# Windowed local attention in a fused attention, mixture-of-heads and MLP kernel: blocks of 64 (or 48) queries against sub-blocks of 32 queries by 64 keys in three of four batches

## Chip, cores and metric

One core of a Trainium2 chip runs the whole program. The metric is the device time of one execution in microseconds (us); the time of a kernel is the median of its runs.

## What is computed

The reference has three stages, all in float32. Only the first is touched here.

```python
def _attn_ref(q, k, v):                      # 4 batches, 8 heads, 576 positions, 64 channels
    scores = scale * np.matmul(q, k.transpose(0, 1, 3, 2))
    rel = pos[:, None] - pos[None, :]
    mask_plain = (rel >= 0) & (rel < 32)                      # heads 0 to 3
    mask_dil = (rel >= 0) & (rel < 128) & (rel % 4 == 0)      # heads 4 to 7
    scores = np.where(mask, scores, -1e9); attn = softmax(scores)
    return np.matmul(attn, v)
```

Its output, 4 x 576 x 512, goes through a layer of four causal heads, of which two per token are kept by a gate (`_moe_ref`), and then through a normalized MLP of width 2048 (`_moe2_ref`).

A plain head looks at the last 32 positions. A dilated head splits the 576 positions into 4 classes (position modulo 4) of 144, and within a class looks at the last 32 as well. So both kinds are a band 32 wide, and a block of n queries needs n + 32 keys.

## The kernel before

**Layout.** Heads are worked in pairs (`hp` 0 to 3; 0 and 1 plain, 2 and 3 dilated), one head on partitions 0 to 63 and the other on 64 to 127. For each batch and pair (16 in all), `load_qk` and `load_v` (L340, L364) issue DMAs from SP, `turned_qk` (L438) turns q and k by TensorE transposes into `qT` and `kT`, `scores` (L491) fills two PSUM banks, and two chains of `window` (L527), one per half `u` of the blocks, do the rest.

**Blocks.** Plain: 9 blocks of 64 queries by 96 keys, five in half 0 and four in half 1. Dilated: 12 blocks of 48 queries by 80 keys, six in each half. A block's scores lie on 64 partitions per head, so a half has 128 partitions by (blocks x keys) columns: 480, 384 or 480.

**Scores (L502 to L525).** First the mask is written into the bank by a bfloat16 product with the identity (L507, L512, L513), then q times k is added (L521). The stationary operand is 64 x 64 (or 64 x 48), and four tiles of the 128 x 128 array are used in turn: two row halves (the heads) by two column halves. Every float32 product appears as two records in the trace, so a plain pair has 36 records on L521 and a dilated one 48.

**Softmax and output (`window`).** For each half: a maximum (L542), exponentials in small ACT instructions, one per block (L551), or by a DVE addition and one large ACT instruction (L545, L548), a sum (L554), a reciprocal (L556), a product (L558, on DVE or POOL), one TensorE transpose per block (L570) in groups of up to four, each group into one bank and copied out by ACT or DVE to `pT` (L573), then the product with v (L587). There the stationary operand is v, 96 x 64 or 80 x 64, the moving one 64 or 48 columns, and the two heads use the two column halves of the array. Last, the result is split into a rounded part `xh` and a rest `xl` (L601, L603).

**Order.** All work is written as chains of Python generators; `run_chains` (L205) picks at each step the operation that could start first by its own table of costs and books it on an engine. So the order of instructions on every engine is fixed when the program is built, and a change of block sizes or of booked costs re-orders work of other stages too. An operation can be offered to two engines (`either`). On PE it books 128 ns more when the tile mode changes (L237). Buffers are places that are taken (`acq`) and given back (`give`): two of `sc` and one of `pT` per half, two of `vt`, eight banks.

**Stages.** Batch 0's local attention fills the first 40 us. From about 48 to 221 us the local attention of batches 1 to 3 is interleaved with the gated heads (`value_tile` L611, `project` L700, `attend` L774) and `out_proj` (L928) of the batch before. The MLP starts when the local attention of batch 3 is done (`open_mlp` L986): its weights are decoded from 221 us on, beside the last gated heads, and from about 320 us its products (L1181, L1203) fill PE.

Of the kernel before, what the change touches and what calls it, by code (L numbers as in the profile page):

```python
# [7 lines left out]
F32 = mybir.dt.float32  # L8
# [9 lines left out]
NEG = -1.0e30  # L18
# [5 lines left out]
def windowed_attention_moe_mlp(  # L24
# [38 lines left out]
    SCALE = 0.125  # L63
    DQ, DW = 48, 80
    LEAN = 0.0
    NBD = S // DQ

    def qrange(i):
# [76 lines left out]
    nc.vector.tensor_copy(mfirst, mgen)  # L145
    nc.vector.memset(mdil[:, 0, 0:W], NEG)
    nc.vector.memset(mfirst[:, 0:W], NEG)

    tri = const.tile([P, E, E], F32, name="tri")
    nc.gpsimd.memset(tri, 1.0)  # L150
# [21 lines left out]
    def acq(tag, n=1):  # L172
        return "acq", tag, n
# [138 lines left out]
    left = {}  # L312
    places.update(nat=[0.0] * 2, vt=[(0.0, LENT), (0.0, 0)], qT=[0.0] * 2, xh=[0.0] * XB)
    for u in range(NU):
        places["sc", u], places["pT", u] = [0.0] * 2, [0.0]
    land = [0.0]

    def last(k, n):
# [42 lines left out]
        LD[b, hp] = nats, times  # L361
        put("ld", b, hp, at=0.0)

    def load_v(b, hp, engines=("SP",)):  # L364
        h0 = 2 * hp
        dil = h0 >= H // 2
        if b == 0 and not dil:
            t, home = 0.0, None
            vt = late(f"vt{b}_{hp}", F32)
        else:  # L370
            t, home = (0.0, 8) if b == 0 and hp == NHP // 2 else (yield acq("vt"))
            if home:
                vt = x2a[:, home:home + 3].rearrange("p a n -> p (a n)")
            else:
                vt = win.tile([P, NBD * 2 * D], F32, tag="vt", name=f"vt{b}_{hp}")
        yield op("POOL", 250.0, [t])
        jobs = []
        if not dil:
            vt = vt[:96, :NBK * 2 * D].rearrange("p (t h d) -> p t h d", t=NBK, h=2)
            nc.gpsimd.memset(vt[0:W, 0], 0.0)  # L380
            jobs.append((32.0, vt[W:96, 0], v[b, h0:h0 + 2, 0:64].rearrange("h p d -> p h d")))
            for h in range(2):
                vs = v[b, h0 + h]
                jobs.append((192.0, vt[:, 1:, h], bass.AP(tensor=vs.tensor, offset=vs.offset + (64 - W) * D,
                                                          ap=[[D, 96], [64 * D, NBK - 1], [1, D]])))
        else:
            vt = vt[:DW, :NBD * 2 * D].rearrange("p (h c n) -> p h c n", h=2, c=3)
            nc.gpsimd.memset(vt[0:W, :, 0], 0.0)
            jobs.append((60.0, vt[W:DW, :, 0], v[b, h0:h0 + 2, 0:4 * DQ].rearrange("h (p r) d -> p h (r d)", r=4)))
            for h in range(2):  # L390
                vs = v[b, h0 + h]
                jobs.append((100.0, vt[:, h, 1:], bass.AP(tensor=vs.tensor, offset=vs.offset + 4 * (DQ - W) * D,
                                                         ap=[[4 * D, DW], [4 * DQ * D, 2], [1, 4 * D]])))
        tv = 0.0
        for x, (kb, dst, src) in enumerate(jobs):
            ns = 800.0 if x == 0 else 660.0
# [85 lines left out]
        put("qT", b, hp, at=max(ends))  # L482


    SC = {u: [win.tile([P, NBD // NU, 97], F32, name=f"sc{u}{x}") for x in range(2)] for u in range(NU)}
    for sx in SC[0] + SC[1]:
        nc.gpsimd.memset(sx[:, :, 96:], 1e-9)
    PSC = {}
    DBLK = (range(0, NBD // 2), range(NBD // 2, NBD))

    def scores(b, hp):  # L491
# [35 lines left out]
    def window(b, hp, u):  # L527

        t = yield key("s1", b, hp)
        tx = yield key("xh", b)  # L530
        xh, xl = XH[b], XL[b]
        dil = 2 * hp >= H // 2
        ts = yield acq(("sc", u))
        ps, psv = [x[u] for x in PSC[b, hp]]
        blk, qw, kw = (DBLK[u], DQ, DW) if dil else (BLK[u], 64, 96)
        nb = len(blk)
        off = 96 - kw
        sx = SC[u].pop(0)
# [21 lines left out]
        tp = yield acq(("pT", u))  # L560
        bw = 2 * qw
        pT = win.tile([96, (5 - u) * P if u == 0 else NBD * DQ], F32, tag=f"pT{u}", name="pT")[:kw]
        ends = []
        pw = 64 + qw
        for a, z in ((0, 3), (3, nb)) if nb > 4 else ((0, nb),):
            ta = yield acq("bank")
            pt = bank("ppt")
            td = yield op("PE", (z - a) * turn(pw), [t, ta])
            for tt in range(a, z):
                nc.tensor.transpose(pt[:kw, P * (tt - a):P * (tt - a) + pw], sc[:pw, tt], ident[:pw, :pw])  # L570
            w = (z - a) * bw
            tc_, e = yield either(("ACT", act(w)), ("DVE", dve(w)), deps=[td, tp])
            copy_by(e, pT[:, bw * a:bw * z].rearrange("p (t n) -> p t n", n=qw),  # L573
                    pt[:kw, :P * (z - a)].rearrange("p (t n) -> p t n", n=64)[:, :, :qw])
            give_bank(pt, tc_)
            ends.append(tc_)
        give(("sc", u), td)
        SC[u].append(sx)
# [11 lines left out]
        give(("pT", u), t)  # L590
        if home is not None and last(("vt", b, hp), NU) and not (b == 0 and home == 8):
            places["vt"].append((t, home))
        n = qw * nb
        if dil:
            pov = po[:, :n].rearrange("p (r j) -> p r j", r=2)
            xv = [x[:, hp].rearrange("p (j r) -> p r j", r=4)[:, 2 * u:2 * u + 2] for x in (xh, xl)]
        else:
            pov, xv = po[:, :n], [x[:, hp, 64 * blk[0]:64 * blk[0] + n] for x in (xh, xl)]
        wide = float(n) if dil else 0.0
# [623 lines left out]
    with tc.manual_schedule():  # L1223
        chain(-20.0, all_loads())
        chain(-19.0, warm())
        for b in range(B):
            for hp in range(NHP):
                chain(b * 10 - 7 - 5.3 + 0.5 * hp, turned_qk(b, hp))
                chain(b * 10 - 3.6 - 7 + 0.5 * hp, scores(b, hp))
                for u in range(NU):  # L1230
                    chain(b * 10 - 3.6 - 7 + 0.5 * hp + 0.1 * u, window(b, hp, u))
# [61 lines left out]
```

## Time and profile before

| | |
|---|---|
| median of 3 runs | 714.37 us (714.24 to 714.5) |
| the profiled execution | 714.91 us, its span 713.2 us |
| PE | 696.9 us busy, 5403 records |
| VectorE (DVE) | 512.4 us busy, 1214 |
| ScalarE (ACT) | 299.4 us busy, 838 |
| GpSimd (POOL) | 169.9 us busy, 198 |
| DMA | 43.12 MB, mean 60 GB/s |

Busy time of PE counts the latency of pipelined matmuls, so two records that overlap, and short gaps between them, both look busy. How long a block of matmuls really holds PE is read from a timeline: from the start of its first record to the start of the first record of whatever follows.

### The profile page before, as it was taken

The page shows a single profiled execution, that of the slowest core. Times are in us where ns is not written, and L with a number is a line of the kernel's source. Part 1 is how long each engine was busy: PE and PEld are TensorE (multiplying, and loading weights), DVE is VectorE, ACT ScalarE, POOL GpSimd, SP SyncE. Part 2 cuts the span into 40 slices and gives each one's busy share as a digit, 9 for nine tenths or more (in the row PEclk, how much of TensorE's full clock was granted, in tenths as well). Part 3 has the DMA queues.
Part 4 walks back from the last instruction along what each step waited for, and adds up shares of the span by engine and source line. Part 5 has one row for each costly group of instructions (what it writes and reads, how often), then busy time and mean ns, then how long its engine had stood idle before and what let it go on. Part 6 is the DMA issues. An engine that isn't in the chain of part 4 may idle for free.

```text
span 713.2 us, 13905 instructions
## 1 busy us (share of the span) xinstructions
PE 696.9 (98%) x5403; PEld 587.0 (82%) x5403; DVE 512.4 (72%) x1214; ACT 299.4 (42%) x838; POOL 169.9 (24%) x198
## 2 busy tenths in 40 slices
PE   7999999999999999999999999999999999999997
PEld 5788898989899887778788888888888888888886
DVE  5659979797987999974788874774864855844343
ACT  4667768576866867731332321211211211211110
POOL 3643122120111132410034440330420511410000
PEclk9899999999999999999999999999999999999999
DMA  9984524053112121100012210110110200100123
GB/s 163 192 161 91 112 49 97 16 123 90 34 25 63 47 68 40 31 29 1 1 60 59 90 64 25 60 60 0 60 59 1 89 30 30 31 0 1 59 89 119
DMA packets 78386, 43.12 MB, mean 60 GB/s; under 512 B 60144, under 2 KB 73712, under 8 KB 78320
## 3 DMA queue, kind: packets, MB, share of 16 engines
q1 hardware_dynamic: 78320, 42.23, 23.5%
q8 instruction: 43, 0.70, 0.4%
q14 instruction: 23, 0.19, 0.1%
HBM read 35.14 MB, written 4.72 MB: 56 GB/s over the span
## 4 chain that ended last, share of the span: by engine, by line
PE 82%; DVE 10%; ACT 4%; issue 2%; DMA 1%; POOL 1%; SPq 0%; DVEq 0%; ACTq 0%; POOLq 0%
PE pout L1203 28%; PE phid L1181 28%; PE pp L728 5%; PE pv L627 3%; PE pwo L953 3%; PE ppt L876 2%; PE po L587 2%; PE ptr L457 2%; PE py L897 2%; PE ppt L570 2%; PE s L521 1%; PE s L800 1%; PE s L801 1%; PE py L895 1%; ACT Pp L816 1%
## 5 line engine op out<-in xcount | busy, mean ns | idle before, releaser
L1203 PE MATMUL pout<-wp,ht 128*128 128x512 f32 x864 | 220.2, 395 | 0.0
L1181 PE MATMUL phid<-xn,wp 128*128 128x512 f32 (+1 forms) x960 | 218.9, 372 | 0.0
L1181 PEld LDWEIGHTS phid<-xn,wp 128*128 128x128 f32 x960 | 168.8, 188 | 34.4
L1203 PEld LDWEIGHTS pout<-wp,ht 128*128 128x128 f32 x864 | 160.0, 188 | 35.1 <-ACT ht L1186 0.2
L1186 ACT ACTIVATE ht<-phid 128x512 fp32r<-128x512 f32 (+1 forms) x80 | 44.3, 554 | 225.0 <-PE phid L1181 224.9
L1212 DVE SCALAR_TENSOR_TENSOR x2a<-pout,rstd,x2a 128x512 f32<-128x512 f32 x124 | 92.5, 747 | 54.9 <-PE pout L1203 54.1
L1188 DVE SCALAR_TENSOR_TENSOR ht<-phid,ht 128x512 fp32r<-128x512 f32 (+1 forms) x80 | 50.8, 635 | 58.5 <-ACT ht L1186 57.8
L1055 POOL TENSOR_TENSOR d_pw<-d_pw,d_t 128x512 f32<-128x512 f32 x32 | 41.4, 1294 | 191.9 <-DVE d_pw L1052 170.4
L1067 POOL TENSOR_TENSOR wp<-d_pw,wp 128x512 fp32r<-128x512 f32 x32 | 42.8, 1339 | 43.2 <-ACT wp L1065 43.2
L558 POOL TENSOR_TENSOR sc<-sc,rs 128x480 f32<-128x480 f32 (+1 forms) x28 | 26.8, 966 | 63.2 <-DVE rs L556 20.2
L1039 ACT ACTIVATE d_sq<-ws 128x512 f32<-128x512 f32 x32 | 21.7, 677 | 44.4 <-DVE d_pw L1058 25.7
L252 ACT COPY pT<-ppt 80x288 f32<-80x288 f32 (+7 forms) x76 | 33.0, 447 | 14.1 <-PE ppt L876 10.0
L816 ACT ACTIVATE Pp<-s,nm 128x64 f32<-128x64 f32 (+3 forms) x64 | 30.6, 479 | 13.0 <-DVE nm L814 10.9
L1065 ACT CAST wp<-d_pw 128x512 fp32r<-128x512 f32 x32 | 19.9, 623 | 35.2 <-DVE d_pw L1058 32.5
L1058 DVE SCALAR_TENSOR_TENSOR d_pw<-d_sq,d_pw 128x512 f32<-128x512 f32 x32 | 22.1, 690 | 15.4 <-POOL d_pw L1055 15.1
L800 PE MATMUL s<-KH,SQ 128*128 128x288 f32 (+4 forms) x96 | 31.2, 330 | 0.1
L551 ACT ACTIVATE sc<-s,mx 128x96 f32<-128x96 f32 (+1 forms) x108 | 26.6, 353 | 11.2 <-DVE mx L542 10.8
L876 PE MATMUL ppt<-ident,Pp 128*128 128x128 f32 x160 | 29.1, 281 | 0.8 <-DVE pT L252 0.5
L1212 DVE SCALAR_TENSOR_TENSOR x2b<-pout,rstd,x2b 128x512 f32<-128x512 f32 x32 | 24.0, 749 | 8.2 <-PE pout L1203 8.0
L1045 DVE SCALAR_TENSOR_TENSOR d_t<-ws,d_t 128x512 int32<-128x512 int32 x32 | 28.7, 896 | 0.4
L801 PE MATMUL s<-klz,SQ 128*128 128x288 f32 (+4 forms) x96 | 28.5, 302 | 0.0
L814 DVE TENSOR_REDUCE nm<-s 128x1 f32<-128x64 f32 (+3 forms) x64 | 25.7, 415 | 3.4 <-PE s L803 2.9
(170 smaller groups left out, 1294.1 us busy)
## 6 DMA issues: line engine op xcount, KB each, us to landing
ws<-in_moe_w_ch_dram SPq DMA_DIRECT2D x32, 512.0 KB, 3.9
nat<-in_q_dram SPq DMA_DIRECT2D x12, 288.0 KB, 4.4
nat<-in_k_dram SPq DMA_DIRECT2D x12, 288.0 KB, 4.8
out_dram<-x2a SPq DMA_DIRECT2D x12, 256.0 KB, 2.0
KH<-KH SPq DMA_DIRECT2D x32, 72.0 KB, 2.0
vt<-in_v_dram SPq DMA_DIRECT2D x10, 192.0 KB, 3.5
x2a<-in_v_dram SPq DMA_DIRECT2D x8, 160.0 KB, 2.5
vt<-in_v_dram SPq DMA_DIRECT2D x8, 160.0 KB, 4.0
```

What stands on the lines that cost most here:

```text
L728: nc.tensor.matmul(pp[:, :HS], ws[:, c, pr_ * P:(pr_ + 1) * P], xs[:, c, cs], start=n == 0, stop=n == 3 * KC - 1)
L800: nc.tensor.matmul(ps[:m, :z - a], SQ[ee][:, q0:q0 + m], KH[ee][:, a:z], start=True, stop=False)
L801: nc.tensor.matmul(ps[:m, :z - a], SQ[ee][:, q0:q0 + m], KL[ee][:, a:z], start=False, stop=not end)
L816: nc.scalar.activation(Pt[:m, :n], pss[0][:m, :n], AF.Exp, bias=nm[:m, ee:ee + 1], accum_out=sm[:m, ee:ee + 1])
L876: nc.tensor.transpose(pt[:, P * (j - 1):P * j], Ps[ee][:, k0:k0 + P], ident)
L1055: nc.gpsimd.tensor_tensor(pf, pf, t1.bitcast(F32), op=ALU.add)
L1067: nc.gpsimd.tensor_tensor(lo, pf, hi.bitcast(F32), op=ALU.subtract)
L1181: nc.tensor.matmul(ph[:, :n_tok], ws[:, c * P:(c + 1) * P], xs[c], start=n == 0, stop=n == 3 * KC - 1)
L1186: nc.scalar.activation(hh[:, :n_tok], ph[:, :n_tok], AF.Relu)
L1188: nc.vector.scalar_tensor_tensor(hl[:, :n_tok], ph[:, :n_tok], 0.0, hh[:, :n_tok].bitcast(F32), op0=ALU.max, op1=ALU.subtract)
L1203: nc.tensor.matmul(po, a_[:, sl], w_, start=n == 0, stop=n == 3 * len(fs) - 1)
L1212: nc.vector.scalar_tensor_tensor(x2(i), po, rstd[:, i:i + 1], x2(i), op0=ALU.mult, op1=ALU.add)
```

## The change

For batches 1 to 3 (`b >= WIDE`, WIDE = 1) the local attention goes in sub-blocks of 32 queries by 64 keys. Plain: 18 sub-blocks of a head, ten in half 0, eight in half 1. Dilated: per class five sub-blocks (the last of 16 queries), 20 of a head, ten in each half. Two neighbouring sub-blocks of both heads lie side by side on 128 partitions (2 heads x 2 x 32 queries), so a half has five (plain half 1: four) columns of 64 keys. Batch 0 keeps its blocks.

- Scores: 8 tiles (64 rows x 32 columns) in turn instead of 4; eight mask products (dilated) and 80 records (plain 72) for a pair.
- `narrow_window` takes the maximum and the exponentials of a half; `narrow_local` takes sum, reciprocal and product of both halves together. 1e-9 is added by its own small instruction, not by an extra column.
- Five transposes of 128 x 128 for a pair: the two halves of a step lie beside each other (2 x 64 keys), so one transpose turns both.
- The product with v: 80 records (plain 72), stationary 64 x 64 on two row halves (`u`) by two column halves (heads), moving 32 columns (16 in a class's last).
- v is loaded with 64 key rows for every 32 queries on two partition halves, by 5 DMAs (plain) or 6 (dilated) instead of 3; no fill of zeros by POOL for dilated pairs.
- Constants: one bfloat16 fill and eight selects on POOL, four copies and four fills on DVE; two fills of `sc` columns on POOL.

```diff
+    NS, WIDE = 5, 1
...
+    mask = win.tile([P, NS, 2 * W], BF16, name="mask")
+    nc.gpsimd.memset(mask[:, 1], 0.0)
+    for x in range(4):
+        m = mask[W * x:W * x + W, 1]
+        nc.gpsimd.affine_select(out=m, in_=m, pattern=[[1, 2 * W]], compare_op=ALU.is_gt,
+                                fill=NEG, base=0, channel_multiplier=-1)
...
+    for x in (0, 2, 3, 4):
+        nc.vector.tensor_copy(mask[:, x], mask[:, 1])
+    for x in range(4):
+        nc.vector.memset(mask[W * x:W * x + W, x % 2 * 2, 0:W], NEG)
...
+    def narrow_jobs(b, h0, dil, vt):
...
+            jobs.append((16.0, vt[W:2 * W, 0], v[b, h0:h0 + 2, 0:W].rearrange("h p d -> p h d")))
+            for u, i0, n in ((0, 1, 9), (1, 0, 8)):
+                for h in range(2):
+                    jobs.append((17.5 * n, vt[64 * u:64 * u + 64, i0:i0 + n, h],
...
+            for u in range(NU):
+                y, o = 64 * u, 2 * u * D
+                for h in range(2):
+                    jobs.append((80.0, vt[y:y + 2 * W, 0:4, h],
...
+                jobs.append((35.0, vt[y:y + m, 4],
...
+    def narrow_scores(b, hp):
...
+        t = yield op("PE", 920.0, [tq, ta], "eighths")
+        tiles = [(u, z, c) for c in range(2) for u in range(NU) for z in HALVES]
+        for u, z, c in tiles:
+            n = parts(dil, u)
+            k = side(u, z).start + W * c
+            o, idn = psv[u][k:k + W], ident_bf[z, z.start + W * c:z.start + W * c + W]
+            if dil:
+                nc.tensor.matmul(o, idn, mask[z], start=True, stop=False)
...
+        for s in range(NS):
+            for u, z, c in tiles:
+                n = parts(dil, u)
+                if s < n:
+                    q0, mq, mk, _ = piece(dil, u, s, c)
+                    k = side(u, z).start + W * c
+                    nc.tensor.matmul(psv[u][k:k + mq, s, :mk], qT[z, q0:q0 + mq], kT[z, q0:q0 + mk],
+                                     start=False, stop=s == n - 1)
...
+    def narrow_local(b, hp):
...
+        t = max((yield key("ex", b, hp, 0)), (yield key("ex", b, hp, 1)))
...
+        nc.vector.tensor_reduce(sm, sf[:, :nb], axis=AX.X, op=ALU.add)
+        t = yield op("DVE*", 75.0, [t])
+        nc.vector.tensor_scalar(sm, sm, 1e-9, None, op0=ALU.add)
...
+        for a, z in ((0, 3), (3, NS)):
...
+            for s in range(a, z):
+                nc.tensor.transpose(pt[:, P * (s - a):P * (s - a + 1)], sx[:, s].rearrange("p u w -> p (u w)"), ident)
...
+        t = yield op("PE", 1170.0, ends + [ta, tv], "quarters")
+        for i in range(2 * NS):
+            for u in range(NU):
...
+                r, g = divmod(i, NS)
+                m, o = (min(W, CLS - W * g), CLS * r + W * g) if dil else (W, W * i)
+                y = slice(64 * u, 64 * u + W + m)
+                for h, z in enumerate(HALVES):
+                    p0 = P * (i // 2) + side(u, z).start + W * (i % 2)
+                    vv = vt[y, g, h, D * r:D * r + D] if dil else vt[y, i, h]
+                    nc.tensor.matmul(pos[u][z, o:o + m], vv, pT[y, p0:p0 + m], start=True, stop=True)
...
-                chain(b * 10 - 3.6 - 7 + 0.5 * hp, scores(b, hp))
+                rank = b * 10 - 3.6 - 7 + 0.5 * hp
+                chain(rank, (scores if b < WIDE else narrow_scores)(b, hp))
+                if b >= WIDE:
+                    chain(rank, narrow_local(b, hp))
```

## Rows read from the trace of the kernel before

**Rows 1.** The page, part 1: busy time of each engine.
```profile
PE 696.9 (98%) x5403; PEld 587.0 (82%) x5403; DVE 512.4 (72%) x1214; ACT 299.4 (42%) x838; POOL 169.9 (24%) x198
```

**Rows 2.** Stretches: length, then PE, PEld, DVE, ACT, POOL busy; PEclk, DMA share, GB/s.
```profile
48.00:100.00 52.00, 50.11 (x758) 45.02 (x757) 45.58 (x140) 36.94 (x120) 13.24 (x22) 1.00 0.47 99
100.00:150.00 50.00, 49.91 (x622) 45.06 (x621) 44.83 (x142) 36.78 (x126) 12.78 (x16) 1.00 0.29 63
150.00:221.00 71.00, 70.88 (x927) 63.83 (x925) 60.63 (x203) 51.27 (x170) 11.54 (x18) 1.00 0.27 68
221.00:320.00 99.00, 97.06 (x731) 80.85 (x727) 90.35 (x286) 66.67 (x197) 25.69 (x21) 1.00 0.13 39
```

**Rows 3.** PE timeline around scores blocks: start us, us, engine, line, operation, form.
```profile
107.03 0.40 PE L507 MATMUL s<-mdil,ident_bf 64*64 64x480 bf16 x4
107.26 1.00 PE L521 MATMUL s<-kT,qT 64*48 64x80 f32 x48
108.19 0.66 PE L876 MATMUL ppt<-ident,Pp 128*128 128x128 f32 x4
...
153.23 0.23 PE L512 MATMUL s<-mfirst,ident_bf 64*64 64x96 bf16 x2
...
153.43 1.02 PE L521 MATMUL s<-kT,qT 64*64 64x96 f32 x36
154.39 0.33 PE L859 MATMUL ph<-ident,Ph 128*128 128x128 f32 x1
```

**Rows 4.** PE timeline around transposes of local blocks.
```profile
112.36 0.49 PE L570 MATMUL ppt<-ident,sc 128*96 128x128 f32 x3
112.61 0.45 PE L800 MATMUL s<-KH,SQ 128*128 128x448 f32 x1
...
113.62 0.60 PE L570 MATMUL ppt<-ident,sc 128*96 128x128 f32 x4
113.98 0.38 PE L800 MATMUL s<-KH,SQ 128*128 128x288 f32 x1
...
121.46 0.45 PE L570 MATMUL ppt<-ident,sc 112*80 112x112 f32 x3
121.69 0.38 PE L728 MATMUL pp<-xh,wkh 128*128 128x288 f32 x1
```

**Rows 5.** PE timeline around products with v.
```profile
115.24 1.22 PE L587 MATMUL po<-pT,vt 96*64 96x64 f32 x36
116.39 0.33 PE L859 MATMUL ph<-ident,Ph 128*128 128x128 f32 x1
...
132.17 1.56 PE L587 MATMUL po<-pT,x2a 80*64 80x48 f32 x48
133.66 0.50 PE L953 MATMUL pwo<-woh,yh 128*128 128x512 f32 x1
```

**Rows 6.** DVE groups by form: busy us, mean ns, then idle before.
```profile
L554 DVE TENSOR_REDUCE sm<-sc 128x6 f32<-128x486 f32 x16 | 10.1, 639 | 0.0
L542 DVE TENSOR_REDUCE mx<-s 128x6 f32<-128x480 f32 x16 | 9.9, 645 | 1.8 <-PE s L521 1.7
...
L814 DVE TENSOR_REDUCE nm<-s 128x1 f32<-128x320 f32 x16 | 7.6, 476 | 0.4 <-PE s L803 0.4
```

**Rows 7.** The chain that ended last, stretch 52 to 68 us.
```profile
54.50 1.03 DVE sm L554 x2
```

**Rows 8.** POOL and DVE timelines of the first microseconds.
```profile
3.78 0.27 POOL L139 TENSOR_SCALAR_AFFINE_SELECT mgen<-mgen 64x96 bf16<-64x96 bf16 x1
8.98 0.12 POOL L446 MEMSET kT<- 128x32 f32 x1 [4.93 <-PE s L521]
...
4.08 0.36 DVE L144 COPY mdil<-mgen 128x80 bf16<-128x80 bf16 x3 [2.30 <-POOL mgen L139]
```

**Rows 9.** SP timeline: DMA issues, start us, us.
```profile
63.34 2.50 SPq L332 DMA_DIRECT2D vt<-in_v_dram  x3
65.94 10.05 SPq L745 DMA_DIRECT2D KH<-KH  x4
```

More of the change, by code (lines that the diff above doesn't have):

```diff
@@ L362, in load_qk, with wide_jobs @@
         put("ld", b, hp, at=0.0)
[L364 to L376, printed above, removed]
+    def wide_jobs(b, h0, dil, vt):
         jobs = []
@@ new lines, in load_v @@
+    def load_v(b, hp, engines=("SP",)):
+        h0 = 2 * hp
+        dil = h0 >= H // 2
+        if b == 0 and not dil:
+            t, home = 0.0, None
+            vt = late(f"vt{b}_{hp}", F32)
+        else:
+            t, home = (0.0, 8) if b == 0 and hp == NHP // 2 else (yield acq("vt"))
+            if home:
+                vt = x2a[:, home:home + 3].rearrange("p a n -> p (a n)")
+            else:
+                vt = win.tile([P, NBD * 2 * D], F32, tag="vt", name=f"vt{b}_{hp}")
+        if b < WIDE:
+            yield op("POOL", 250.0, [t])
+            vt, jobs = wide_jobs(b, h0, dil, vt)
+        else:
+            if not dil:
+                yield op("POOL", 250.0, [t])
+            vt, jobs = narrow_jobs(b, h0, dil, vt[:, :4 * NS * D])
@@ L482, in turned_qk @@
         put("qT", b, hp, at=max(ends))
-    SC = {u: [win.tile([P, NBD // NU, 97], F32, name=f"sc{u}{x}") for x in range(2)] for u in range(NU)}
-    for sx in SC[0] + SC[1]:
+    ST = [win.tile([P, NBD * 97], F32, name=f"sc{x}") for x in range(2)]
+    SC = {u: [(x, st.rearrange("p (u t w) -> p u t w", u=NU, w=97)[:, u]) for x, st in enumerate(ST)] for u in range(NU)}
+    for st in ST:
+        nc.gpsimd.memset(st[:, 9 * 2 * W:NS * 4 * W], 0.0)
+    for _, sx in SC[0] + SC[1]:
         nc.gpsimd.memset(sx[:, :, 96:], 1e-9)
-    PSC = {}
+    PSC, SX, SN, wide_end = {}, {}, [], {}
     DBLK = (range(0, NBD // 2), range(NBD // 2, NBD))
@@ L598, in window, with parts @@
             pov, xv = po[:, :n], [x[:, hp, 64 * blk[0]:64 * blk[0] + n] for x in (xh, xl)]
+        wide = float(n) if dil else 0.0
+        th = (yield op("ACT", act(n) + 0.3 * wide, [t, tx])) + 0.6 * wide
+        nc.scalar.copy(xv[0], pov)
+        tl = yield op("DVE", dve(n) + 0.5 * wide, [th])
+        nc.vector.tensor_tensor(xv[1], pov, xv[0].bitcast(F32), op=ALU.subtract)
+        give_bank(po, tl)
+        if last(("x", b, hp), NU):
+            put("x", b, hp, at=tl)
+    def parts(dil, u):
+        return NS if dil or u == 0 else NS - 1
@@ new lines, in piece @@
+    def piece(dil, u, s, c):
+        i = 2 * NS * u + 2 * s + c
+        if not dil:
+            return W * i, W, 2 * W, 2 * W * s + W * c
+        r, g = divmod(i, 5)
+        m = min(W, CLS - W * g)
+        return CLS * r + W * g, m, m + W, CLS * (r % 2) + W * g
+    def narrow_scores(b, hp):
+        tq = yield key("qT", b, hp)
+        qT, kT = TQ[b, hp]
+        dil = 2 * hp >= H // 2
+        ta = yield acq("bank", NU)
+        banks = [bank("s1") for _ in range(NU)]
+        psv = [ps[:, :2 * W * parts(dil, u)].rearrange("p (t w) -> p t w", w=2 * W) for u, ps in enumerate(banks)]
+        t = yield op("PE", 920.0, [tq, ta], "eighths")
[6 more added lines that the diff above has]
+                nc.tensor.matmul(o, idn, mask[z], start=True, stop=False)
+            else:
+                f = 0 if u else 1
+                if f:
+                    nc.tensor.matmul(o[:, 0], idn, mask[z, 0], start=True, stop=False)
+                nc.tensor.matmul(o[:, f:], idn, mask[z, 1, None, :].to_broadcast([64, n - f, 2 * W]),
+                                 start=not f, stop=False)
+        for s in range(NS):
[6 more added lines that the diff above has]
+                                     start=False, stop=s == n - 1)
+        give("qT", t)
+        PSC[b, hp] = banks, psv
+        put("s1", b, hp, at=t)
@@ new lines, in narrow_window @@
+    def narrow_window(b, hp, u):
+        t = yield key("s1", b, hp)
+        ts = yield key("sx", b, hp)
+        dil = 2 * hp >= H // 2
+        ps, psv = [x[u] for x in PSC[b, hp]]
+        nb, kw = parts(dil, u), 2 * W
+        sc = SX[b, hp][:, :nb, u]
+        mx = win.tile([P, NS], F32, tag="nmx", name="nmx", bufs=4)[:, :nb]
+        t = yield op("DVE", dve(kw * nb), [t])
+        nc.vector.tensor_reduce(mx, psv, axis=AX.X, op=ALU.max, negate=True)
+        t, e = yield either(("DVE", dve(kw * nb), 0.0), ("ACT", nb * 198.0, LEAN), deps=[t, ts])
+        if e == "DVE":
+            nc.vector.tensor_tensor(sc, psv, mx[:, :, None].to_broadcast([P, nb, kw]), op=ALU.add)
+            give_bank(ps, t)
+            t = yield op("ACT", act(kw * nb, False), [t])
+            nc.scalar.activation(sc, sc, AF.Exp)
+        else:
+            for s in range(nb):
+                nc.scalar.activation(sc[:, s], psv[:, s], AF.Exp, bias=mx[:, s:s + 1])
+            give_bank(ps, t)
+        put("ex", b, hp, u, at=t)
@@ new lines, in narrow_local @@
+    def narrow_local(b, hp):
+        ts = yield acq("sc")
+        sx = SN.pop(0)
+        SX[b, hp] = sx
+        put("sx", b, hp, at=ts)
+        t = max((yield key("ex", b, hp, 0)), (yield key("ex", b, hp, 1)))
+        dil = 2 * hp >= H // 2
+        nb, kw = parts(dil, 0) + parts(dil, 1), 2 * W
+        sf = sx.rearrange("p s u w -> p (s u) w")
+        sm, rs = [win.tile([P, NS * NU], F32, tag=x, name=x, bufs=2)[:, :nb] for x in ("nsm", "nrs")]
+        t = yield op("DVE", dve(kw * nb), [t])
+        nc.vector.tensor_reduce(sm, sf[:, :nb], axis=AX.X, op=ALU.add)
+        t = yield op("DVE*", 75.0, [t])
+        nc.vector.tensor_scalar(sm, sm, 1e-9, None, op0=ALU.add)
+        t0 = yield op("DVE", 85.0, [t])
+        nc.vector.reciprocal(rs, sm)
+        tp = yield acq("pT")
+        pT = win.tile([P, NS * P], F32, tag="pT", name="pT", bufs=2)
+        ends = []
+        for a, z in ((0, 3), (3, NS)):
+            n = min(NU * z, nb) - NU * a
+            t, e = yield either(("DVE*", dve(kw * n)), ("POOL*", 20.0 + 2.1 * kw * n), deps=[t0])
+            (nc.vector if e == "DVE" else nc.gpsimd).tensor_tensor(
+                sf[:, NU * a:NU * a + n], sf[:, NU * a:NU * a + n],
+                rs[:, NU * a:NU * a + n, None].to_broadcast([P, n, kw]), op=ALU.mult)
+            ta = yield acq("bank")
+            pt = bank("ppt")
+            td = yield op("PE", (z - a) * turn(P), [t, ta])
+            for s in range(a, z):
+                nc.tensor.transpose(pt[:, P * (s - a):P * (s - a + 1)], sx[:, s].rearrange("p u w -> p (u w)"), ident)
+            w = (z - a) * P
+            tc_, e = yield either(("ACT", act(w)), ("DVE", dve(w)), deps=[td, tp])
+            copy_by(e, pT[:, P * a:P * z], pt[:, :w])
+            give_bank(pt, tc_)
+            ends.append(tc_)
+        give("sc", td)
+        SN.append(sx)
+        yield key("lv", b, hp)
+        vt, tv, home = LV[b, hp]
+        ta = yield acq("bank", NU)
+        pos = [bank("po") for _ in range(NU)]
+        t = yield op("PE", 1170.0, ends + [ta, tv], "quarters")
+        for i in range(2 * NS):
+            for u in range(NU):
+                if i // 2 >= parts(dil, u):
+                    continue
+                r, g = divmod(i, NS)
[5 more added lines that the diff above has]
+                    nc.tensor.matmul(pos[u][z, o:o + m], vv, pT[y, p0:p0 + m], start=True, stop=True)
+        give("pT", t)
+        places["vt"].append((t, home))
+        for u in range(NU):
+            chain(b * 10 - 10.6 + 0.5 * hp + 0.1 * u, rounded(b, hp, u, pos[u], t))
```

53 lines of the change are left out of this document (44 added, 9 removed).

## Prediction

> **What bounds the kernel now.** I read the busy times first: PE is busy for 696.9 of 713.2 us [rows 1]. Busy time overlaps, so the second view is the stretches [rows 2]. The reader is to see that PE leaves almost nothing idle from 100 to 221 us (0.09 of 50 us, 0.12 of 71 us), that it has 1.89 us idle from 48 to 100 us, and that its clock is at the upper of its two levels (2.4 GHz, shown as 1.00) in all four. So in 100 to 221 us a microsecond that PE doesn't need is a microsecond gained, as long as other work is there to close up. The third view is the PE timeline, where I take the time from a block's first record to the first record of whatever follows [rows 3 to 5]; only this says what a block costs. The last is the chain that ended last: between 52 and 68 us it runs through DVE, through this very softmax [rows 7].
>
> The change touches 12 head pairs, 6 plain and 6 dilated, all between 48 and 221 us.
>
> **Scores.** Now a dilated pair holds PE from 107.03 to 108.19, 1.16 us: 0.23 for the mask and 0.93 for 48 records, which go round four tiles, so 12 rounds of 77.5 ns. A plain pair takes 153.23 to 154.39, 1.16 us as well, of it 0.96 for 10 rounds of 96 ns [rows 3]. The rounds follow the moving columns: 16 columns more cost 18.5 ns. After the change a pair has 10 rounds of eight tiles with 64 columns, and its mask products have 320 columns for 480, so 0.23 x 2/3 = 0.155 us. The round of eight is not in the trace. Low end: columns alone, 77.5 - 18.5 = 59 ns. High end: eight tiles cost two rounds of four, 155 ns. I take 77.5 ns, the round of the nearest row, since twice as many instructions go into a round while the columns fall by a fifth. That gives 0.155 + 0.775 = 0.93 us, 0.23 less for each of 12 pairs: **2.8 us gained** (ends: 12 x 0.415 = 5.0 gained; 12 x 0.545 = 6.5 lost).
>
> **Transposes.** A plain pair has groups of 3, 2 and 4: 3 take 0.25 us, 4 take 0.36 (0.09 each, so 2 take 0.18), together 0.79. A dilated pair has four groups of 3 at 0.23, 0.92 us [rows 4]. After: one group of 3 and one of 2, 0.25 + 0.18 = 0.43. Gain 6 x 0.36 + 6 x 0.49 = **5.1 us**. If groups had run together at 0.09 or 0.08 each before, the gain is 6 x (0.81 - 0.45) + 6 x (0.96 - 0.45) = 5.2, so this term is firm.
>
> **Product with v.** A plain pair holds PE for 1.15 us, 36 records on two tiles, 18 rounds of 64 ns; a dilated one for 1.49, 24 rounds of 62 ns [rows 5]. The moving columns are 64 in the one and 48 in the other, the stationary operand 64 columns in both, and the round is nearly the same: here it goes with what stays the same, the stationary operand. After the change the stationary operand still has 64 columns, and there are 20 rounds of four tiles. At 63 ns that is 1.26 us. Gain 6 x (1.49 - 1.26) - 6 x (1.26 - 1.15) = **0.7 us**. Low end: the round halves with the moving columns, 31.5 ns, 0.63 us, gain 6 x 0.52 + 6 x 0.86 = 8.3. High end: the two row halves take turns, 126 ns, 2.52 us, loss 6 x 1.37 + 6 x 1.03 = 14.4. I take 63, because four tiles of two row halves do share a round in the scores [rows 3].
>
> PE together: 2.8 + 5.1 + 0.7 = **8.6 us**.
>
> **DVE.** A dilated pair's two maxima of 480 columns cost 1.29 us and two sums 1.28. A reduction of 320 columns costs 476 ns, so a column costs (645 - 476) / 160 = 1.06 ns [rows 6]. After: two maxima 0.95, one sum of 640 columns 645 + 160 x 1.06 = 0.81. That is 0.8 us less, for a plain pair nearly as much; about 9 us of DVE in all, and copies of `pT` and exponentials shrink as well. One reciprocal falls away and one small addition comes. From 100 us on this lies beside PE and I cost it at nothing. From 48 to 100 us DVE is on the chain [rows 7]; PE had 1.89 us idle there, and I leave that as a rival, not in the sum.
>
> **Waits.** The product for both halves now waits for both halves' exponentials, and one place of `pT` serves the pair. Behind it on PE stand projections and gated heads, which the planner puts in between. I cost it at nothing; without such work a pair would lose about the one reduction by which its halves are apart, 0.65 us [rows 6].
>
> **Prologue.** Eight selects at 0.27 us and three small fills are about 2.6 us of POOL; DVE gets eight small instructions, about 0.9 us by the 0.12 of L144. POOL is idle for 4.93 us before 8.98 [rows 8], which covers its part. Without that cover the first scores come up to 2.6 + 0.9 = 3.5 us late. I take 0, and keep 3.5 as the end.
>
> **DMAs.** v grows from 416 to about 611 KB for a plain pair by the shapes in the diff, for a dilated one from 426 to 622. Over 12 pairs that is 2.3 MB at a DMA share of 0.27 to 0.47 [rows 2]: hidden. On SP three issues hold the queue for 2.50 us at worst, 0.83 each, so 5 or 6 of them hold it 1.7 to 2.5 us longer, and behind them stand the copies of `KH` for the gated heads, as at 65.94 [rows 9]. What hides it is other PE work while `KH` is late. The fill of zeros that a dilated `vt` needed goes away.
>
> **Sum.** The profiled execution is 714.91 us, so 714.91 - 8.6 = 706.3. It lies 0.5 us above the median of 714.37; against that the forecast is **705.8 us**.
>
> **The rivals.** *More than PE.* The lighter softmax also takes waits out of 48 to 100 us. For it: the chain runs through DVE there [rows 7]. Against: PE idles only 1.89 us in that stretch, though gaps inside its busy time may hide as much again. It gives up to 3 us more, 702.8.
>
> *SP gives part back.* In each of three batches one late load pushes `KH` copies, and PE runs out of other work: 3 x 2.1 = 6 us at the worst, some 4 likely, 709 to 712. For it: SP's queue is in order [rows 9]. Against: the DMA shares. A planner that orders other stages worse would look the same in the time.
>
> *Slower: the tiles don't overlap.* One mechanism: more tiles don't run at once than do today. Scores then take 0.155 + 1.55 = 1.71 us and the product 2.52, so 12 x 0.545 + 14.4 - 5.1 = 15.8 us slower, 730. With the other terms as forecast it decides when the product's round passes about 99 ns: 7.9 us over 12 pairs are 0.66 us, on 1.32 today, so 1.98 / 20. Against: 48 records in 0.93 us are 19.4 ns apart [rows 3], which one tile after another could not do at 80 columns. The Trainium skill has a rule that would do the same ("TensorE: Matmul & The Clock Gate", section "Wait — 56ns, not 53.3ns?"): start to start never falls below about 25 ns, however few the columns. By it 80 records are 2.0 us, in scores and product alike, and the time would be about 729. The trace disagrees, with 19.4 ns for records that go to different tiles; by that row alone I keep this rival small.
>
> *Nothing arrives.* The order changes, and what PE saves ends as waits elsewhere: 713 to 715.8.
>
> **How the numbers follow.** Forecast (703.5 to 708): 0.58. More than PE (below 703.5): 0.14. Part given back (708 to 712.9): 0.16. Nothing: 0.04. Slower: 0.08. The first three are faster: 0.88. A measurement of this kernel can tell about 0.2%, 1.4 us, from no change. The range 701.5 to 711.5 leaves out slower, nothing, and a quarter each of the two beside the forecast, about 0.2 in all.
>
> **What would show it.** In the profile after, a local pair's scores should hold PE for about 0.93 us, its five transposes 0.43, its product with v 1.26. DVE's sum should appear once for a pair at about 0.8 us. PE's idle time from 48 to 221 us should not grow, and the local attention of batch 3 should end about 8 us before 221. Scores above 1.2 us or a product above 2 us would prove the forecast wrong, and so would PE waits on `KH` or `vt`, or an MLP that starts earlier but ends no earlier.

## The result, and the profile after

The changed kernel takes 723.35 us (720.85 to 724.34, 6 runs) against 714.18 us of the kernel before beside it: ratio 1.0122, 95% interval 1.0104 to 1.0139. It is slower by 1.2%; the prediction was faster by 1.2%.

The page of the kernel after, part 1, answers to [rows 1]:

```profile
PE 692.6 (96%) x6213; PEld 581.0 (80%) x6213; DVE 509.0 (70%) x1228; ACT 288.4 (40%) x802; POOL 153.1 (21%) x189
```

The profiled execution has a span of 722.6 us against 713.2. PE's busy time fell by 4.3 us, and its idle time rose from 713.2 - 696.9 = 16.3 to 722.6 - 692.6 = 30.0: 13.7 more, less 4.3, are the 9.4 us of the span. So PE does have less to do, but it stands still for longer. Where it does so is told by the stretches (columns as in [rows 2]; the last two are stretches of the lower clock):

```profile
48.00:100.00 52.00, 45.17 (x1018) 39.75 (x1018) 40.97 (x138) 35.58 (x118) 9.08 (x17) 0.97 0.45 95
100.00:150.00 50.00, 48.83 (x763) 44.15 (x762) 38.24 (x129) 29.75 (x100) 2.83 (x6) 1.00 0.35 84
150.00:221.00 71.00, 68.14 (x1151) 60.05 (x1149) 57.81 (x200) 44.54 (x149) 5.65 (x12) 1.00 0.32 76
221.00:320.00 99.00, 94.58 (x853) 79.57 (x853) 91.68 (x282) 64.76 (x191) 23.72 (x19) 0.98 0.14 40
...
81.30:84.70 3.40, 3.40 (x18) 2.65 (x17) 2.16 (x9) 1.58 (x6) 0.00 (x0) 0.50 0.84 191
231.50:234.90 3.40, 3.40 (x56) 3.09 (x54) 2.57 (x11) 1.05 (x4) 0.00 (x0) 0.50 0.54 155
```

From 48 to 320 us PE idles 15.3 us where it idled 4.0 [rows 2]; 6.8 of it from 48 to 100 us, where batch 1's local attention runs. In three stretches (the third from 43.7 to 47.2) it also works at the lower of its two levels, 1.2 GHz, for some 3.4 us each; before the one at 81.3 it had stood still for 2.1 us. (The kernel before has one such stretch, of 6.8 us from 15.2 us on, in batch 0, and none later.) The chain that ended last says what it stood still for:

```profile
51.68 0.68 PE s L711 x41
52.36 1.95 issue
54.30 0.40 PE s L711 x13
...
69.94 0.60 SPq L347
70.54 0.04 issue
70.58 0.62 SPq L347
71.20 0.04 issue
71.24 0.60 SPq L347
71.85 0.46 issue
72.30 0.85 SPq L347
73.16 0.07 issue
73.22 6.55 DMA nat<-in_k_dram
```

These are two different things. At 73.22 a load of k is under way that was issued only after a row of DMAs for v (SP's queue, L347). At 52.36 PE stops for 1.95 us in the middle of one block of scores, for nothing that the profile shows ("issue"): no semaphore, no buffer. The waits of PE (line, releaser: us in total, times, longest) name the same two:

```profile
PE s L711 <- issue: 2.6, 2, 1.9
...
PE ptr L508 <- DMA nat<-in_k_dram: 2.1, 1, 2.1
PE ptr L508 <- DMA nat<-in_q_dram: 1.8, 2, 1.0
```

A wait of PE marked "issue" inside a block does not exist in the kernel before. The cause of the late loads (`nat`) is shown by SP's timeline, which answers to [rows 9]: q and k stand behind six DMAs for v, which hold the queue for 5.30 us.

```profile
66.54 5.30 SPq L347 DMA_DIRECT2D x2a<-in_v_dram  x6
72.30 0.85 SPq L347 DMA_DIRECT2D nat<-in_q_dram  x1
73.22 0.82 SPq L347 DMA_DIRECT2D nat<-in_k_dram  x1
74.16 4.90 SPq L347 DMA_DIRECT2D vt<-in_v_dram  x6
```

The blocks themselves, from PE's timeline, to be held against [rows 3 to 5]:

```profile
59.26 0.99 PE L711 MATMUL s<-kT,qT 64*32 64x64 f32 x80 [1.07 <-ACT kT L266]
60.18 0.55 PE L770 MATMUL ppt<-ident,sc 128*128 128x128 f32 x3
...
93.52 0.55 PE L770 MATMUL ppt<-ident,sc 128*128 128x128 f32 x3
93.83 0.34 PE L1012 MATMUL s<-KH,SQ 128*128 128x192 f32 x1
...
94.27 0.21 PE L702 MATMUL s<-mask,ident_bf 64*32 64x64 bf16 x2
...
94.41 0.96 PE L711 MATMUL s<-kT,qT 64*32 64x64 f32 x72
95.30 0.44 PE L770 MATMUL ppt<-ident,sc 128*128 128x128 f32 x2
95.49 0.39 PE L1012 MATMUL s<-KH,SQ 128*128 128x320 f32 x1
...
96.29 1.35 PE L793 MATMUL po<-pT,vt 64*64 64x32 f32 x80
97.57 0.33 PE L1071 MATMUL ph<-ident,Ph 128*128 128x128 f32 x1
```

Scores: 80 records hold PE for 0.92 us, a plain pair with its mask for 95.30 - 94.27 = 1.03. Transposes: 0.31 for three and 0.19 for two (other groups, depending on what stands behind them, 0.25 to 0.42 and 0.14 to 0.31). Product with v: 1.28, for 80 records as for the 72 of a plain pair. DVE's sum (groups by form) comes once for a pair, at about the 0.8 us expected:

```profile
L752 DVE TENSOR_REDUCE nsm<-sc 128x10 f32<-128x640 f32 x6 | 4.9, 815 | 1.4 <-ACT sc L733 1.3
L752 DVE TENSOR_REDUCE nsm<-sc 128x9 f32<-128x576 f32 x6 | 4.5, 746 | 0.2 <-ACT sc L733 0.2
```

### The profile page after: what moved, and what is told of

Same layout as the page of the kernel before. It is cut to its first block, busy times and chain, and to the rows that moved or that the text cites. A ratio compares the mean times of both kernels' runs of the same rounds, so it can differ in the third digit from the quotient of the medians.

```text
span 722.6 us, 15535 instructions
## 1 busy us (share of the span) xinstructions
PE 692.6 (96%) x6213; PEld 581.0 (80%) x6213; DVE 509.0 (70%) x1228; ACT 288.4 (40%) x802; POOL 153.1 (21%) x189
## 2 busy tenths in 40 slices
DMA packets 87128, 45.28 MB, mean 63 GB/s; under 512 B 64080, under 2 KB 82448, under 8 KB 87056
## 4 chain that ended last, share of the span: by engine, by line
PE 79%; DVE 11%; ACT 3%; DMA 2%; SPq 2%; issue 2%; POOL 1%; POOLq 0%; DVEq 0%; ACTq 0%
PE pout L1415 28%; PE phid L1393 27%; PE pp L940 4%; PE pwo L1165 2%; PE pv L839 2%; PE ppt L1088 2%; PE po L793 2%; PE py L1109 2%; PE ptr L508 2%; DVE nm L1026 1%; SPq L347 1%; PE py L1107 1%; PE s L1012 1%; PE s L1013 1%; DVE Pp L1063 1%
## 5 line engine op out<-in xcount | busy, mean ns | idle before, releaser
L1251 ACT ACTIVATE d_sq<-ws 128x512 f32<-128x512 f32 x32 | 21.5, 673 | 43.7 <-DVE d_pw L1270 25.1
L266 ACT COPY pT<-ppt 128x384 f32<-128x384 f32 (+5 forms) x69 | 28.9, 427 | 19.3 <-PE ppt L1088 12.8
L1270 DVE SCALAR_TENSOR_TENSOR d_pw<-d_sq,d_pw 128x512 f32<-128x512 f32 x32 | 22.0, 689 | 14.8 <-POOL d_pw L1267 14.6
L763 POOL TENSOR_TENSOR sc<-sc,nrs 128x384 f32<-128x384 f32 (+2 forms) x16 | 11.9, 750 | 79.7 <-DVE yl L1126 29.5
L1257 DVE SCALAR_TENSOR_TENSOR d_t<-ws,d_t 128x512 int32<-128x512 int32 x32 | 26.6, 831 | 0.4
L839 PE MATMUL pv<-wvh,xh 128*128 128x260 f32 x80 | 24.7, 309 | 0.3 <-DVE xl L815 0.3
```

Of the source, the lines that this page charges most:

```text
L839: nc.tensor.matmul(pv[:, :NV], xs[:, c, q0:q0 + P], ws[:, c], start=c == 0 and n == 0, stop=c == KC - 1 and n == 2)
```

## The experiments

Ratios are to the kernel before on the same chip. Its median was 714.84 us beside w4_none, w3_one, w2_two and qk_first; 713.95 beside qk_shift144, after_shift96, qk_spaced and w2_spaced; 714.78 beside before_shift144, qk_shift256 and spaced_shift80. So kernels of different groups are compared by their ratios. "Theory A" in the expectations is the late loads, "Theory B" that PE runs dry of instructions.

### How many batches, and the order of loads

`WIDE` says from which batch on the sub-blocks are used; the constants are built in any case. In w4_none it is 4 (no batch), in w3_one 3 (the last batch), in w2_two 2 (the last two).

```diff
-    NS, WIDE = 5, 1
+    NS, WIDE = 5, 4
```

> WIDE = 4: no batch uses the sub-blocks; the new constants, the shared sc and pT buffers and the new order of the booking stay. Theory A (the loss is made by the loads of v and by what stands behind them on SP, batch by batch): 714, as before. Theory B (PE runs dry of instructions in the dense new blocks): 714 too, no PE stall inside a local block. Rival C (the shared buffers or the constants cost it): 717 or more.

Measured: 715.19 us, 0.9999 (0.9985 to 1.0013). The constants and their prologue cost nothing that can be told.

> WIDE = 3: only batch 3 in sub-blocks. The loss of all three is 9.2 us. Theory A: the first narrow batch sets off most of it, since all v loads of a batch are late only against the batch's own q and k; a third, about 717, or less because batch 3 has no local attention behind it. Theory B: about a third of the stalls inside blocks, 1 to 2 us, 715 to 717. Rival C: 720 or more already.

Measured: 715.14 us, 1.0003 (0.9983 to 1.0023).

> WIDE = 2: batches 2 and 3 in sub-blocks, batch 1 as before. In the trace of after batch 1 ends 13 us late and batches 2 and 3 add little. Theory A: if batch 1 is the place of the loss (v of 6 DMAs ahead of q and k of its last pair, PE waits 2.1 and 0.8 us on them), then 714 or better, perhaps 711 to 714. Theory B: two thirds of the stalls, so 717 to 720.

Measured: 713.26 us, 0.9967 (0.9943 to 0.9991). Two batches gain 0.3%, and with batch 1 added the kernel is 1.2% slower, so batch 1 costs some 11 us. One batch alone gains nothing: in w3_one PE idles 71 - 69.14 = 1.86 us from 150 to 221 us, 0.12 before. The 713.26 lies where the late loads (Theory A) put it and below Theory B's 717 to 720: the stalls are not spread evenly over the batches.

In the fourth kernel all three batches are narrow, but q and k of the next pair are issued ahead of v of this one, so that no v DMA stands in front of them:

```diff
         for b in range(1, B):
             yield from room(b)
+            yield from load_qk(b, 0)
             for hp in range(NHP):
-                yield from load_qk(b, hp)
+                if hp + 1 < NHP:
+                    yield from load_qk(b, hp + 1)
                 yield from load_v(b, hp)
```

> All three batches in sub-blocks; q and k of the next pair are issued ahead of v of this one. Theory A: PE's waits on nat (3.9 us) go, and with them the half clock behind them at 82 us: 717 to 719. Theory B: those waits are not the main thing, 721 to 724, with the stalls inside blocks (some 5 us) unchanged.

Measured: 722.21 us, 1.0108 (1.007 to 1.0146). The waits on `nat` are gone, and the time is hardly shorter. Its PE waits show what came instead:

```profile
PE s L713 <- issue: 4.9, 3, 2.5
PE po L795 <- issue: 2.6, 2, 2.0
...
PE py L1109 <- issue: 1.0, 1, 1.0
```

These three lines are 8.5 us, where the changed kernel had 2.6. So taking the late loads away gains next to nothing here, because waits without a releaser took their place.

### The stalls without a wait

I counted PE's instructions in order (weight loads, matmuls, semaphores) in all traces so far, and listed every gap over 0.45 us, from start to start, that follows no semaphore:

```
kernel    instruction (us)                          
after     1472 (52.14 to 54.30), 6080 (189.58 to 190.43), 6336 (192.77 to 194.18)
w3_one    5056 (1.56)
w2_two    2752 (99.54 to 101.33), 5312
qk_first  1728 (52.75 to 55.48), 3520, 4800, 5312 (154.71 to 156.93), 6080, 7104
before, w4_none: none
```

Each of these numbers is 192 more than a multiple of 256. (The view of waits books the gap at 192.77 on a copy by ACT, `pTh`; that ended at 193.4, and PE went on 0.8 us later.) And the page's DMA queues have one for instructions, the first line from the kernel before, the second from the one after:

```profile
q8 instruction: 43, 0.70, 0.4%
```

```profile
q8 instruction: 49, 0.80, 0.5%
```

Each packet has 16,384 bytes, and PE's instructions number 10,959 before and 12,573 after: 255 and 257 for a packet. **New theory:** PE's instructions come in packets of 256, and it stalls where it has used one up before the next has come. The kernel before takes 5.9 to 12.8 us for a packet from 48 to 221 us. The narrow blocks hold 312 (plain) to 336 PE instructions of scores and product with v for a pair, against 156 to 200, some 5.6 ns apiece in the scores; two pairs' scores side by side use a packet in 1.4 us, as at 52 us.

If so, a program of the same order must change its time when all of it is shifted against the packets' edges. The warm-up, seven large products that nothing uses, serves for that: the same planned place, but more and smaller instructions (each product is a weight load and a matmul). PE's instructions behind it are the same, in the same order. This is the edit of qk_shift144:

```diff
-        for _ in range(7):
-            nc.tensor.matmul(b.rearrange("p (x n) -> p x n", n=P), ident_bf,
-                             ident_bf[:, None].to_broadcast([P, 4, P]), start=True, stop=True)
+        for _ in range(79):
+            nc.tensor.matmul(b[:16, :44], ident_bf[:, :16], ident_bf[:, :44], start=True, stop=True)
```

79 products for 7 are 144 more instructions. qk_shift256 is qk_first with 256 more, after_shift96 the changed kernel with 96, before_shift144 the kernel before with 144.

> The kernel of qk_first with 144 more short PE instructions in the warm-up and nothing else changed. Theory B (PE's instructions come in packets of 256, and a packet can't be used up in under some 3.4 us, so PE stands still at a packet's edge inside dense blocks): every edge moves by 144 records. Applying 3.4 us to the trace of qk_first, the stalls at edges there sum to 9.7 us, and with the shift to 3.6 us: about 6 us faster than qk_first, 716, stalls near 53.5 and 129 us of its old times, none in the product with v near 154. Rival A (the stalls are waits on data, loads or semaphores): same 722, stalls at the same work as before.

Measured: 712.89 us, 0.9971 (0.9951 to 0.9991), 1.4% below qk_first and better than expected. PE's waits without a releaser fell from 8.5 to 2.6 us. The gain, 1.4% or 9.8 us, is larger than these 5.9. The lower clock accounts for the rest as far as an estimate goes: from 48 us on qk_first has four stretches of 3.4 us at 1.2 GHz, three of them at or within 0.9 us of the end of a stall of 1.7 to 2.7 us, and qk_shift144 has one; three stretches at half the rate are up to 5.1 us. Of the two stalls foretold, the one at 53 us came, and the one near 129 didn't: there a packet was used in 2.4 us without a stall, so the 3.4 us that the expectation worked with are no fixed limit. Here is one stretch, first in qk_first, then in qk_shift144:

```profile
55.30:58.70 3.40, 3.21 (x76) 3.07 (x76) 1.68 (x5) 2.02 (x9) 0.70 (x2) 0.50 0.46 124
```

```profile
55.30:58.70 3.40, 3.26 (x41) 3.02 (x41) 2.47 (x6) 2.08 (x9) 0.00 (x0) 1.00 0.60 165
```

Both had just stood still, for 2.5 and 2.2 us; in qk_first the clock fell to 1.2 GHz, in the other it didn't. Why, no run tells.

> The changed kernel with 96 more short PE instructions in the warm-up and nothing else changed. Theory B: the stall of 2.2 us in the first scores at 52 us goes; two stalls of about 2 us each remain or appear, in the dense blocks near 118 and 188 us; 1 to 2 us faster than after, 721 to 722.5. Rival A: 723, the stall at 52 us stays.

Measured: 718.07 us, 1.0052 (1.0035 to 1.007): 0.7% (5.0 us) below the changed kernel, more than expected. The stall at 52 us is gone, and two remain, at 115 and 185 us; the gaps at edges fell from 4.4 to 2.7 us. PE's waits on `nat` fell too, from 3.9 to 0.6 us, though the loads have the same order: so late loads and edges can't be taken apart in that kernel.

> The kernel before with the same small warm-up as qk_shift144 (144 more PE instructions ahead of everything, nothing else touched). Theory (the loss sits where PE crosses from one packet of 256 instructions to the next too soon): the kernel before crosses every edge with 5.8 to 15 us to spare and has no stall, so there is nothing to move: 714 us, ratio 0.998 to 1.002, no PE wait marked issue. Rival (the other warm-up itself is what won 9.3 us between qk_first and qk_shift144): this kernel wins as much, about 705 us, ratio 0.987.

Measured: 714.77 us, 1.0003 (0.9992 to 1.0013), and no wait of PE without a releaser. The small warm-up itself gains nothing; where there is no stall, a shift does nothing.

> qk_first with 256 more PE instructions in the warm-up, a whole packet, so every edge falls on the same instruction of the attention as in qk_first without them. Theory (packet edges): the stalls come back at the same places (the largest, 2.7 us, in the first scores of batch 1, at about 53 us) and the time is qk_first's, 720 to 724 us, ratio 1.008 to 1.014. Rival (the small warm-up as such, or a chance order of the DMAs behind it, won the 9.3 us of qk_shift144): 712 to 714 us.

Measured: 719.78 us, 1.0078 (1.0053 to 1.0103), just below the 720 to 724 expected and far from the rival's 712 to 714. Shifted by a whole packet, the stalls are back at the same instructions. The same product with v, in qk_first and then in qk_shift256, both stopped after its 71st record:

```profile
153.69 1.25 PE L795 MATMUL po<-pT,vt 64*64 64x32 f32 x71
156.93 0.31 PE L795 MATMUL po<-pT,vt 64*64 64x32 f32 x9 [2.00 <-issue]
```

```profile
154.47 1.25 PE L794 MATMUL po<-pT,vt 64*64 64x32 f32 x71
158.27 0.31 PE L794 MATMUL po<-pT,vt 64*64 64x32 f32 x9 [2.55 <-issue]
```

Last the cost by itself, away from any attention: 512 small products in eight tiles and two banks as the warm-up of the kernel before.

```diff
-        for _ in range(7):
-            nc.tensor.matmul(b.rearrange("p (x n) -> p x n", n=P), ident_bf,
-                             ident_bf[:, None].to_broadcast([P, 4, P]), start=True, stop=True)
+        for i in range(512):
+            c = 32 * (i // 2 % 4)
+            nc.tensor.matmul((b, b2)[i % 2][c:c + 32, :64], ident_bf[HALVES[i % 2], :32],
+                             ident_bf[HALVES[i % 2], :64], start=True, stop=True)
```

> The disputed cost by itself: the kernel before, its warm-up of 7 products replaced by 512 small bfloat16 products (32 stationary, 64 moving columns, eight tiles in turn), 1,024 PE instructions with no wait among them and no attention around them. Theory (a packet of 256 instructions takes some 3.1 to 3.7 us to be brought): the block crosses four edges, stalls at 192, 448, 704 and 960 instructions unless packets lie ready at the start, each marked issue, with successive stalls at least 3.1 us apart, and takes 10 to 14 us. Rival (the stalls belong to the attention's place: its loads, its PSUM banks, its softmax): no wait marked issue, about 5.6 ns an instruction as in a block of 80 scores, 5.7 us, or up to twice that at the lower clock. The time as a whole says nothing here: the first scores start later by what the block is longer.

Measured, in a single execution (PE's timeline; the time as a whole was 724.23 us beside 715.6, by the longer start):

```profile
1.83 2.40 PE L415 MATMUL warm<-ident_bf 64*32 64x64 bf16 x223 [1.83 <-DVE ident_bf L93]
7.97 1.27 PE L415 MATMUL warm<-ident_bf 64*32 64x64 bf16 x128 [3.75 <-issue]
12.52 1.28 PE L415 MATMUL warm<-ident_bf 64*32 64x64 bf16 x128 [3.28 <-issue]
16.25 0.44 PE L415 MATMUL warm<-ident_bf 64*32 64x64 bf16 x33 [2.45 <-issue]
```

This is the mechanism laid bare: 128 products, 256 instructions, run in 1.28 us, and then PE waits for the next 256. From one packet to the next it takes 4.55 and 3.73 us. The clock was at its upper level here throughout. The first edge, at 192, made no stall: that packet had been there from the start, and only from 448 on do they come one by one. The block took 14.8 us, a little above what was expected.

The traces also hold the start and the length of every packet of q8, and these show the theory directly. Each kernel has as many packets as its PE program has edges at 192 and every 256 on: 43 before, 49 after, 46 here. For the three stalls above and the one at 52 us of the changed kernel (us):

```
kernel, edge         packet on its way    PE goes on
before_dense, 448    5.17 to 6.46         7.97
before_dense, 704    10.12 to 11.04       12.52
before_dense, 960    13.65 to 14.88       16.25
after, 1472          51.69 to 52.82       54.30
```

In all traces of this case there are 33 stalls of over 0.45 us at an edge. In each of them PE goes on 1.2 to 1.7 us after its packet has landed, and no other edge of the 14 traces is crossed earlier than 1.3 us after. The time from edge to edge is less regular, since a packet sets out at different times. In the changed kernel PE used one packet in 2.1 us (117.5 to 119.6) without a stall, for the one behind it had set out early, at 117.31. In qk_spaced, below, PE stalled at 79 us although its packet had lasted 6.7 us, for the one behind had set out only 5.1 us after the packet's start. What makes a packet set out, no run tells.

### Spacing the dense blocks

If density is the cause, two pairs' scores should not follow each other. For every second pair the scores wait, in the planner, for the exponentials of the pair before:

```diff
     def narrow_scores(b, hp):
         tq = yield key("qT", b, hp)
+        if hp % 2:
+            tq = max(tq, (yield key("ex", b, hp - 1, 1)))
```

qk_spaced adds this to qk_first, w2_spaced to w2_two; spaced_shift80 is qk_spaced with the warm-up's shift, at a place chosen so that few edges fall into dense blocks.

> qk_first, and the scores of the second pair of two wait until the exponentials of the first are booked, so that two dense blocks no longer touch. Theory B: the stalls at packet edges fall from 8.5 us to below 4: 717 to 719. Rival (the loss in batch 1 is the order of the work and not the stalls): 721 or more.

Measured: 710.36 us, 0.9949 (0.9923 to 0.9975): far better than expected, faster than both kernels. Four stalls remain, 4.4 us of gaps from start to start where qk_first has 9.8, and from 48 us on there is no stretch of the lower clock where qk_first has four. The edit also re-orders the program, so the edges lie elsewhere as well; what the spacing is worth without that isn't shown.

> Batches 2 and 3 in sub-blocks with the same spacing of the scores. Theory B: the one stall of 1.8 us near 100 us goes: 711 to 712. Rival: order alone decides, 713 or more.

Measured: 717.12 us, 1.0042 (1.0021 to 1.0063): a miss; by the ratios it is 0.75%, some 5.4 us, slower than w2_two. The stall at 100 us that it was made for is gone, but the edit re-orders the program, and three edges (3264, 4288, 6080) now fall into dense blocks, 3.6 us of waits without a releaser against 1.9. That is 1.7 of the 5.4 us, and neither kernel has the lower clock from 48 us on; the rest is open. Spacing alone is no cure while the edges lie by chance.

> qk_spaced with 80 more PE instructions in the warm-up. Laying edges 256 instructions apart over qk_spaced's own times, with at least 3.4 us from one to the next, makes 4.1 us of stalls at its own place and 1.6 us at this one. Theory (packet edges): 2.5 us faster than qk_spaced, 706 to 709 us, ratio 0.989 to 0.993. Rival (what is left over qk_spaced's PE time is no matter of the edges): 710.4 us, as qk_spaced.

Measured: 708.51 us, 0.9919 (0.9905 to 0.9934), the best of all and within its expectation. Its stretches, and the one stall that is left:

```profile
48.00:100.00 52.00, 49.77 (x1077) 45.40 (x1076) 43.86 (x146) 38.42 (x137) 9.21 (x18) 1.00 0.50 116
100.00:150.00 50.00, 49.73 (x844) 44.13 (x843) 43.32 (x140) 35.34 (x116) 9.96 (x15) 1.00 0.28 69
150.00:221.00 71.00, 70.41 (x1178) 62.94 (x1178) 59.28 (x204) 47.76 (x161) 6.79 (x11) 1.00 0.34 80
```

```profile
PE s L714 <- issue: 1.3, 1, 1.3
```

From 48 to 221 us PE idles 2.2 + 0.3 + 0.6 = 3.1 us, near the 2.1 of the kernel before [rows 2], and the clock stays up there. Its PE is busy for 689.0 us, 7.9 less than before, with 40 more products in the warm-up.

### Load order and edges side by side

The four kernels make a square of ratios:

```
                       edges as they fell    shifted
v ahead of q and k     1.0122  after         1.0052  after_shift96
q and k ahead of v     1.0108  qk_first      0.9971  qk_shift144
```

Shifting is worth 0.7% with the one order and 1.4% with the other; the order is worth 0.1% with the edges as they fell and 0.8% shifted. The new order alone shows next to nothing, and its stalls are longer, 9.8 us of gaps against 4.4. Only the two kernels of a row have the same program of PE, but for the warm-up. Down a column the order of loads re-plans PE's program, and 96 and 144 are different shifts, so what the order is worth by itself isn't shown.

## Why the prediction was wrong, step by step

**What bounds the kernel.** Right: PE, and a microsecond less of PE was to be a microsecond gained "as long as other work is there to close up". What was missing is a condition that no view of the kernel before could show failing: that PE's instructions come as fast as it runs them. They number 15% more after the change, and where they are dense, PE waits for them: gaps of 4.4 us at three edges in the changed kernel and 9.8 at six in qk_first. This is the step that failed. I counted twice as many instructions into a round of the scores and asked only what they cost the array. The stalls are not the whole 9.2 us: waits on late loads (3.9 us) and two stretches of the lower clock from 48 us on go with them, and how the loss divides among the three isn't shown. That they can be taken away together is: order of loads, spacing and shift bring the ratio from 1.0122 to 0.9919.

**Scores.** The round of eight tiles is 0.92 / 10 = 92 ns (forecast 77.5; ends 59 and 155). A dilated pair takes 1.05 us (from 152.24 to 153.29 in PE's timeline), a plain one 1.03, so the gain is 6 x 0.11 + 6 x 0.13 = 1.4 us instead of 2.8. Mis-sized: it follows neither the columns nor the nearest row alone.

**Transposes.** By the rows shown, 0.31 + 0.19 = 0.50 us a pair for 0.43: 0.8 us less gain, 4.3. The term was called firm, but what a group holds PE for depends on what stands behind it.

**Product with v.** 1.28 us for 1.26: right, though a plain pair has 72 records, 18 rounds and not 20, and takes as long. The gain is 0.5 us. The terms of PE therefore come to some 6.2 us instead of 8.6, and spaced_shift80 is 0.0081 x 714.78 = 5.8 us faster than the kernel before. So the mechanism behind the forecast exists, and what took it away is elsewhere. That the two figures lie so close is in part luck, since spaced_shift80 also has another order of loads and scores and still one stall.

**DVE.** Right: one sum a pair, 0.75 to 0.82 us, and nothing comes of it.

**Waits.** Costed at nothing; the transposes wait 2.1 us in all on the product of the softmax (POOL 1.7, DVE 0.4 us). No run isolates it.

**Prologue.** Nothing that can be told, as w4_none shows.

**DMAs and SP.** Called hidden; this failed too. That v's issues hold SP longer was sized well: 6 of them take 4.90 to 5.30 us against 2.50 for 3, 2.4 to 2.8 us more (forecast 1.7 to 2.5). The bytes grew by 45.28 - 43.12 = 2.16 MB, near the 2.3 forecast; a plain pair's v grows from 426 to 573 KB by its shapes, and the 416 and 611 were the planner's bookings. But I looked for `KH` copies behind them, and what came late was q and k of the next pair: 3.9 us of waits in PE. A step that lengthens a queue must be followed to every load behind it.

**The rivals.** *The tiles don't overlap* is false: 80 records in 0.92 us are 11.5 ns apart. By an estimate from the 25 ns of the Trainium skill ("TensorE: Matmul & The Clock Gate", section "Wait — 56ns, not 53.3ns?") they would take 2.0 us; the measurement disagrees for records that go to different tiles. The kernel came out slower, but through none of the mechanisms listed. *SP gives part back* happened, on `nat` instead of `KH`; what it is worth alone isn't shown. The signs I named spoke: PE's idle time from 48 to 221 us grew from 2.1 to 10.9 us, the last product with v ended at 235.6 us instead of 220.6, and the first product of the MLP started at 264.4 instead of 246.7.

## What to carry to other kernels

When a change cuts matmuls into smaller ones, count PE's instructions in the densest stretch as well as their time: here no packet of 256 was used up in less than 2.0 us without a stall, and in a stall the next mostly came 2.2 to 4.6 us after the last. Such waits show mostly as "issue" in the middle of a block. Two things tell them from everything else: a shift of the whole program by some instructions, which should change nothing, and the landing of the instruction packets, if the trace has it. Before two kernels of different order are compared to within 1%, it is worth knowing where those edges fell.

## What the runs showed of the hardware that was not expected

PE's program is brought in packets of 16,384 bytes, 256 instructions. Run without any other wait, 256 small instructions took 1.28 us and the next packet let PE go on 3.73 to 4.55 us after the last one had. The 4.55 us are 2.15 until the packet sets out, 0.92 on its way and 1.48 until PE goes on. In the attention the stalls were 0.6 to 2.7 us. The edge lies at the same count, 192 and every 256 on, in every kernel. Stretches of 3.4 us at 1.2 GHz come behind some of these stalls, behind a late load as well, and not behind others as long; what decides that stays open. From 48 us on there are four in qk_first and in qk_shift256, two in the changed kernel and in after_shift96, one in qk_shift144, and none in the kernel before or in qk_spaced. Open too is how a plan should know the edges beforehand: the place of spaced_shift80 was chosen from a trace.
